# Attention times a token-mixing gate on one core: four closing adds moved to GpSimd, a clearing moved to VectorE, and another PSUM bank for the last span's sums

## The chip, the cores and the metric

The kernel runs on one core of a Trainium2 chip. The metric is the device time of one launch, in microseconds (us): the median of three timed runs was 1622.77 us before the change (1622.52 to 1623.23). The engines are TensorE (PE in the profile; its weight loads are PEld), VectorE (DVE), ScalarE (ACT), GpSimd (POOL) and the queue of SyncE (SP), from which nearly all transfers are started.

## What is computed

With S = 2048 tokens, D = 512 channels, 32 heads of 16 channels and a hidden size F = 1792 (all float32):

```python
xn = layernorm(x)
q, k, v = split(xn @ wqkv)                      # 32 heads of 16
s = concat_heads(softmax(q @ k.T * 16**-0.5) @ v) @ wo
h = layernorm(xn)
u = gelu(einsum("bsd,sf->bdf", h, w1) + b1)     # mixes tokens
y = einsum("bdf,fs->bds", u, w2) + b2
return x + s * silu(y.T)
```

## The kernel before the change

**Stages.** The first 200 us or so normalise x, make q, k and v, and begin the mixer. Then comes one long stretch in which attention and the mixer share TensorE. Attention runs over 16 pairs of heads; a pair has two spans of 1024 queries, and a span has 16 blocks of 128 keys. For each unit (a pair, a span and a key block) there are first row maxima (`max_of`, L524: a product on 48 rows, then a reduction on VectorE), and 22 units later the scores (`score`, L964): four products of 50 rows into a PSUM bank each, two for each head `a`, and ScalarE's exponential of each bank into a `prob` tile. Two units later `values` (L978) multiplies the unit's four `prob` tiles by the values (eight matmuls in the profile, 1 us in all) into one bank that sums over the 16 key blocks of a span; that bank's tile is `state["av"]`. `put_away` (L718) copies it to SBUF at the span's end. The two heads use the two halves of TensorE's rows, so their products run side by side.

**The fill.** Everything else that TensorE has to do is made by generators (`mixer`, L575, and `rest`, L995) that yield one product at a time, and a pair (work, give the bank back) at the end of each sum. `take(n, each)` (L1069) draws n of them for each step. Between yields the generators also start weight loads (`w_load`), split weights into two parts on GpSimd (`w_split`, L165 and L95) and load the mixer's results; so when a generator is advanced decides where these stand in their queues. Before the change `take` looked one item ahead after its last product, to see whether the end of a sum came next, and so advanced the generator then.

**The last 70 us.** When the last row maxima are done (`s == NU`, L1259, about 1550 us), the banks for scores (four) and for maxima (three) become one list of seven free banks, `Banks.free`. `Banks.tile` takes the first bank of the list and puts it at the end at once, so tiles rotate through what is on the list and a tile waits for the readers of the one that had the bank before; `Banks.hold` takes the first bank off the list until its second result, `back`, is called. The eighth bank is `ps_av`, in which the spans' sums stood. From there on each loop step has two half-steps (`a_half`, L1162): four scores, up to three products of the fill on each half of the rows, and then the values of an earlier unit. The fill's sums (tiles named `dn`) hold a bank each. The last products of the output projection (L1010 and on) finish the first eight of 16 blocks of rows in this stretch: `finish` (L953) multiplies a projection sum by the gate and adds the earlier part of the sum, y, on VectorE, and stores it. The pair's first span is turned with eight TensorE transposes (`own`, L831: L843 and L854, four each, into a `mx` bank).

**The close.** The last span's sums are copied by ScalarE (L725), turned (L1368), divided on VectorE into the cleared buffer `apart[0]` (`uo`, cleared by `clear_apart`, L869), turned back (`turn_back`, L1385), and split (`upper`, `lower`). Then come the last eight blocks, 8 to 15, in the order of `half`: 8, 9, 12, 13, 10, 11, 14, 15. For each, `product` (L1403) has three TensorE products, `gated` (L1409) multiplies by the gate, and `added` (L1411) adds y and stores. Block 15 goes in two halves (`in_parts`, L1419).

Blocks 8 and 9 (`SUMMED`) were different: their y was written straight to the output earlier (`store_y`, L911), and the gated sum was added to it there by a transfer started from GpSimd that accumulates (L1414). The y of the other blocks goes to `y_d` and comes back by `load_second` (L921, the transfer at L929) into `held`.

Of the kernel before, what the change touches and what calls it, by code (L numbers as in the profile page):

```python
# [9 lines left out]
F32 = mybir.dt.float32  # L10
F32R = mybir.dt.float32r
AF = mybir.ActivationFunctionType
OP = mybir.AluOpType
# [9 lines left out]
def tile_attention_token_mixer(ctx, tc, x, wqkv, wo, w1, b1, w2, b2, out):  # L23
    nc = tc.nc
    P = 128
# [4 lines left out]
    NP = H // 2  # L30
    NB = S // P
# [3 lines left out]
    QH = S // 1024  # L35
# [30 lines left out]
    ps_sc = Banks("ps_sc", 4)  # L66
    ps_mx = Banks("ps_mx", 3)
    ps_av = Banks("ps_av", 1)
# [649 lines left out]
    def put_away(p, span, av):  # L718

        ev = el.tile([P, 512], F32, name="ev")  # L720
        if p == NP - 1 and span < QH - 1:

            nc.vector.tensor_copy(ev, av)  # L723
        else:
            nc.scalar.copy(ev, av)  # L725
        if p == NP - 1:
            own(span, ev)
            return
        g, i = divmod(p, 4)
        if i == 0:  # L730
            dens[span] = sm.tile([P, 64], F32, name="d")
        rows = ev.rearrange("(j r) q -> r j q", r=32)
        for a in range(2):
            h = 2 * i + a
            nc.sync.dma_start(
                dens[span][DH * h : DH * (h + 1), :],
                rows[16 - 16 * a, 2 * a : 2 * a + 2, :].rearrange("c (j q) -> c j q", q=64),
            )
        nc.sync.dma_start(num_d[g][span][160 * i : 160 * i + P, :], ev)
        if i == 3 or p == NP - 2:  # L740
            invert(g, span)
# [125 lines left out]
    apart = []  # L867

    def clear_apart():  # L869

        apart.append(el.tile([P, 2, 512], F32, name="uo"))
        nc.gpsimd.memset(apart[0], 0.0)

    xts = {}
    gts = {}
# [1 line left out]
    gates = {}  # L877
    held = []
    PARTS = NB - 2
    LATE = NB - 4  # L880
    HALVES = 5
    SUMMED = range(NB // 2, NB // 2 + 2)

    def load_part(b):

# [7 lines left out]
    def part(b, ps):  # L893

        y = el.tile([P, D], F32, name="t", bufs=4)
        late = now[0] >= NU - 2
        if late:
            nc.vector.tensor_tensor(out=y, in0=ps, in1=gts[b], op=OP.mult)
        else:
            nc.scalar.copy(y, ps)  # L900

        def two():
            if not late:
                nc.gpsimd.tensor_tensor(out=y, in0=y, in1=gts[b], op=OP.mult)
            nc.gpsimd.tensor_tensor(out=y, in0=y, in1=xts[b], op=OP.add)
            load_part(b + 2)
            after(3, lambda: store_y(b, y))

        after(2, two)

    def store_y(b, y):  # L911
        if b in SUMMED:
            nc.sync.dma_start(out[b * P : (b + 1) * P, :], y)
            return
        nc.sync.dma_start(y_d[b], y)
        if b >= NB // 2:
            unkept.append(b)
# [3 lines left out]
    def load_second():  # L921

        b = next((b for b in unkept if b >= PARTS), min(unkept))
        unkept.remove(b)
        i = b - NB // 2
        while len(held) < NB // 8:
            held.append(big.tile([P, S], F32, name="big"))
        ys[b] = held[i // 4][:, i % 4 * 512 : i % 4 * 512 + 512]
        nc.sync.dma_start(ys[b], y_d[b] if b < PARTS else xv[:, b, :])  # L929
# [31 lines left out]
    state = {}  # L961
# [16 lines left out]
    def values(t):  # L978
        p, r = divmod(t, SPP)
        span, kb = divmod(r, NB)  # L980
        if kb == 0:
            state["av"] = ps_av.tile([P, 512], F32, name="av")
        av = state["av"]
        for a in range(2):
            for c in range(2):
                j = 2 * a + c
                nc.tensor.matmul(  # L987
                    av[32 * j : 32 * j + 32, :],
                    vps[p][:, kb, 16 * a : 16 * a + 32], prob.pop((t, a, c)),
                    start=kb == 0, stop=kb == NB - 1,  # L990
                )
        if kb == NB - 1:
            soon.append(lambda: put_away(p, span, av))
# [46 lines left out]
    def everything():  # L1040
        yield from mixer()
        yield from rest()

    class Fill:
# [10 lines left out]
        def next(self):  # L1055
            x = self.peek()
            self.ahead.clear()
            return x

    fill = Fill(everything())  # L1060
    open_ = True
# [7 lines left out]
    def take(n, each):  # L1069

        nonlocal open_, done
        got = 0
        while open_ and (got < n or fill.peek() and len(fill.peek()) == 2):
            x = fill.next()
            if x is False:
                open_ = False
            elif x is None:
                break
            elif len(x) == 2:
                def then(empty, back):  # L1080
                    empty()
                    back()

                each(None, lambda x=x: then(*x))
                if fill.peek() is None:
                    fill.next()
                    break
            else:
                each(x, None)
                got += 1  # L1090
        done += got

    def whole(x, then):
# [111 lines left out]
    def both_pairs(s, keep):  # L1205
# [5 lines left out]
        for i, kinds in enumerate((*zip(first, second), "")):  # L1211
# [14 lines left out]
            if then and not two:  # L1226
                then.pop()()

    take(FIRST, whole)
    after(5, lambda: load_v(0))  # L1230
    if NP > 1:
# [13 lines left out]
    def keep(s):  # L1245

        if done >= n_fill // 2 + 3 * NF:
            divisions()
        if s >= NU - SPP + LEAD and unkept:
            load_second()  # L1250

    for s in range(0, total + 1, 2):
# [16 lines left out]
        elif s < NU and t >= 0:  # L1269
# [6 lines left out]
            for i, kinds in enumerate((*zip(first, second), "")):  # L1276
                if i in places:

                    if i == places[0]:
                        piece()  # L1280
                    now[0] = s + places.index(i)
                    if now[0] >= LEAD + 2:
                        values(now[0] - LEAD - 2)
                    run_later()
                for of, kind in zip(made, kinds):
                    if of[kind]:
                        of[kind].pop(0)()
# [18 lines left out]
        else:  # L1306
# [13 lines left out]
            if s == NU + 16:  # L1320
                clear_apart()
# [9 lines left out]
        if 0 <= t < NT:  # L1331
            p, r = divmod(t, SPP)
# [23 lines left out]
    def some(n):  # L1356
        for f in beside[:n]:
            f()
        del beside[:n]
# [13 lines left out]
    for c in range(2):  # L1373
        for a in range(2):
            j = 2 * a + c
            nc.vector.tensor_tensor(
                out=spread[:, c, :, 96 + DH * a : 112 + DH * a], in0=turned[:, :, j, DH * a : DH * a + DH],
# [12 lines left out]
    def lower(h, c):  # L1390
        o = oc[ND - 1, 2 + c][96:, :, 256 * h : 256 * h + 256]
        sub(nc.vector, o[:, 1, :], back[h, c][96:, :256], o[:, 0, :])
# [3 lines left out]
    def product(n):  # L1396
        b = half[n]
        new = b not in sums
        if new:
            sums[b] = (ps_av if n == 0 else ps_sc).tile([P, 512], F32, name="av" if n == 0 else "sc")[:, :D]  # L1400
        o, at = oc[ND - 1, b // 4], cols[b % 4]
        for m, w in ((0, 0), (0, 1), (1, 0)):
            nc.tensor.matmul(sums[b], o[:, m, at], wide[w], start=new and m == 0 and w == 0, stop=m == 1)  # L1403

    def gated(n):
        b = half[n]
        g = gates[b]
        gates[b] = pp.tile([P, 512], F32, name="prob")[:, :D]
        nc.vector.tensor_tensor(out=gates[b], in0=sums[b], in1=g, op=OP.mult)  # L1409

    def added(n, eng):  # L1411
        b = half[n]
        if b in SUMMED:
            nc.gpsimd.dma_start(out[b * P : (b + 1) * P, :], gates[b], accum_op=OP.add)  # L1414
            return
        eng.tensor_tensor(out=gates[b], in0=ys[b], in1=gates[b], op=OP.add)
        nc.sync.dma_start(out[b * P : (b + 1) * P, :], gates[b])

    def in_parts(n):  # L1419
        b = half[n]  # L1420
        to = pp.tile([P, 512], F32, name="prob")[:, :D]
        for at in (slice(0, D // 2), slice(D // 2, D)):
            nc.vector.tensor_tensor(out=to[:, at], in0=sums[b][:, at], in1=gates[b][:, at], op=OP.mult)
            nc.vector.tensor_tensor(out=to[:, at], in0=ys[b][:, at], in1=to[:, at], op=OP.add)
            nc.sync.dma_start(out[b * P : (b + 1) * P, at], to[:, at])
# [11 lines left out]
        turn_back(1, c)  # L1437
        upper(1, c)
    lower(1, 0)
    adding = {0: [0], 1: [1], 3: [2], 4: [3], 5: [4], 6: [5, 6]}  # L1440
    for n in range(8):
        if n > 5:
            some(len(beside) if n == 7 else len(beside) - 9)
        product(n)
        if n == 7:
            in_parts(n)
            break
        gated(n)
        for i in adding.get(n, ()):
            added(i, nc.gpsimd if i in () else nc.vector)  # L1450
        if n == 1:
            lower(1, 1)

# [26 lines left out]
```

## Time and profile before

| what | us |
|---|---|
| median of three timed runs | 1622.77 |
| the profiled execution, its own time | 1621.93 |
| its span | 1620.0 |
| TensorE busy in the span | 1610.4 |
| VectorE busy | 1414.3 |
| ScalarE busy | 1192.3 |
| GpSimd busy | 552.4 |

The granted clock was 0.999 over the span. The profiled execution's own time is 1.93 us over its span and 0.84 us under the median of the runs. A row of the timeline has the start, the duration, the engine, the line, the operation and the tiles (out<-in), and in brackets the idle time before it with what ended that. Rows of matmuls have their shape as rows used by columns. Matmuls are pipelined: in a stream they start 0.23 us apart on each half of the rows, while each row says 0.39 us or more.

### The profile page before, as it was taken

Reading aid. Unit: us, or ns where it says so; the run is one execution under the profiler, and the core shown is the slowest. Engines: PE = TensorE matmul, PEld = TensorE weight load, DVE = VectorE, ACT = ScalarE, POOL = GpSimd, SP = SyncE. Lnnn points to the kernel's source line nnn. Section 1 sums busy time; section 2 is a strip of 40 time slices with the busy share of each in tenths; the row PEclk is TensorE's granted clock in tenths of the full one; section 3 lists DMA queues with packets and bytes.
Section 4 is the critical chain, followed back from the end, with each engine's and each line's share of the span. In section 5 each row is a group of like instructions: output and inputs, shape, how many; then the busy total and the mean of one; then the engine's idle time right before and its main releaser. Section 6 shows DMA issues by size and latency. Waiting matters only on the chain.

```text
span 1620.0 us, 31089 instructions
## 1 busy us (share of the span) xinstructions
PE 1610.4 (99%) x11899; PEld 876.2 (54%) x11899; DVE 1414.3 (87%) x2478; ACT 1192.3 (74%) x2306; POOL 552.4 (34%) x651
## 2 busy tenths in 40 slices
PE   9999999999999999999999999999999999999998
PEld 8888854554555554554454554544555545554544
DVE  7665999999999999999999999999999999999945
ACT  3333477777777777777877787777877777888885
POOL 1224844342244332332333332223232322563330
PEclk9999999999999999999999999999999999999999
DMA  7478441515133141826151522304150614444346
GB/s 231 178 249 200 120 93 41 96 39 78 41 68 75 27 79 40 241 71 109 41 83 37 85 59 42 69 31 76 38 86 31 113 32 80 112 99 131 111 136 222
DMA packets 151120, 153.34 MB, mean 95 GB/s; under 512 B 51372, under 2 KB 109996, under 8 KB 147900
## 3 DMA queue, kind: packets, MB, share of 16 engines
q1 hardware_dynamic: 146524, 150.25, 38.6%
q0 software_dynamic: 4448, 1.12, 0.5%
q8 instruction: 93, 1.52, 0.4%
q14 instruction: 55, 0.45, 0.1%
HBM read 99.63 MB, written 50.58 MB: 93 GB/s over the span
## 4 chain that ended last, share of the span: by engine, by line
PE 97%; DVE 1%; POOL 0%; issue 0%; ACT 0%; DMA 0%; SPq 0%; POOLq 0%; DVEq 0%
PE av L987 31%; PE dn L1132 23%; PE sc L971 17%; PE mx L533 14%; PE sc L436 3%; PE dn L672 2%; PE mx L436 2%; DVE mxp L537 1%; PE av L436 1%; PE dn L1178 0%; PE sc L104 0%; PE sc L102 0%; PE sc L103 0%; PE mx L340 0%; PE mx L102 0%; PE mx L104 0%
## 5 line engine op out<-in xcount | busy, mean ns | idle before, releaser
L537 DVE TENSOR_REDUCE mxp<-mx 128x1 f32<-128x512 f32 x2026 | 1250.3, 682 | 112.0 <-PE mx L533 85.7
L976 ACT ACTIVATE prob<-sc 128x512 f32<-128x512 f32 x2004 | 1039.7, 607 | 282.3 <-PE sc L971 116.5
L533 PE MATMUL mx<-big 48*128 48x512 f32 x2026 | 769.5, 419 | 0.1
L971 PE MATMUL sc<-big 50*128 50x512 f32 x2004 | 733.6, 412 | 0.5 <-ACT prob L976 0.5
L987 PE MATMUL av<-prob,vp 128*32 128x512 f32 x4096 | 545.5, 604 | 0.3 <-DVE ev L723 0.2
L1132 PE MATMUL dn<-hu,wh 64*128 64x512 f32 x1520 | 506.2, 404 | 0.0
L971 PEld LDWEIGHTS sc<-big 50*128 50x128 f32 x2004 | 353.9, 186 | 230.4 <-ACT prob L976 205.6
L533 PEld LDWEIGHTS mx<-big 48*128 48x128 f32 x2026 | 356.7, 185 | 196.0 <-DVE mxp L537 173.8
L1132 PEld LDWEIGHTS dn<-hu,wh 64*128 64x128 f32 x1520 | 272.1, 184 | 68.2 <-issue 45.3
L1132 PE MATMUL dn<-hu,wl 64*128 64x512 f32 x762 | 301.9, 396 | 0.0
L987 PEld LDWEIGHTS av<-prob,vp 128*32 128x32 f32 x4096 | 80.9, 108 | 176.3 <-issue 164.0
L95 POOL TENSOR_TENSOR wl<-raw,wh 128x512 fp32r<-128x512 f32 x124 | 150.7, 1218 | 64.0 <-ACT wh L167 22.6
L165 POOL CAST wh<-raw 128x512 fp32r<-128x512 f32 x104 | 60.4, 581 | 277.0 <-PE dn L1132 114.5
L1132 PEld LDWEIGHTS dn<-hu,wl 64*128 64x128 f32 x762 | 140.5, 184 | 11.6
L561 POOL CAST m<-f 16x128 fp32r<-16x128 f32 x31 | 8.7, 280 | 240.7 <-DVE f L549 240.7
L99 POOL DMA_DIRECT2D big<-m x124 | 65.6, 536 | 0.0
L622 POOL TENSOR_TENSOR sq<-u 128x512 f32<-128x512 f32 x11 | 11.5, 1041 | 133.7 <-ACT u L616 133.7
L1132 PE MATMUL dn<-wh,hu 64*128 64x512 f32 x144 | 51.0, 407 | 0.0
L709 POOL TENSOR_SCALAR t<-t 128x512 f32<-128x512 f32 x16 | 23.8, 1488 | 79.6 <-ACT t L706 79.5
L436 PE MATMUL sc<-xt,big 128*128 128x512 f32 x184 | 44.5, 390 | 0.0
L95 POOL TENSOR_TENSOR hu<-hx,hu 128x512 fp32r<-128x512 f32 x16 | 20.4, 1294 | 68.5 <-ACT hu L279 68.5
L672 PE MATMUL dn<-hu,wh 64*128 64x512 f32 x128 | 42.3, 392 | 0.0
(224 smaller groups left out, 1180.6 us busy)
## 6 DMA issues: line engine op xcount, KB each, us to landing
raw<-in_B_w_dram SPq DMA_DIRECT2D x104, 256.0 KB
big<-k_d SPq DMA_DIRECT2D x96, 128.0 KB
big<-q_d SPq DMA_DIRECT2D x96, 128.0 KB
q_d<-sg SPq DMA_DIRECT2D x16, 512.0 KB
k_d<-sg SPq DMA_DIRECT2D x16, 512.0 KB
num_d<-ev SPq DMA_DIRECT2D x30, 256.0 KB
u_d<-uo SPq DMA_DIRECT2D x14, 512.0 KB
hu<-u_d SPq DMA_DIRECT2D x14, 512.0 KB
```

Of the source, the lines that this page charges most:

```text
L95: eng.tensor_tensor(out=o, in0=a, in1=b.bitcast(F32), op=OP.subtract)
L99: queue.dma_start(dst.bitcast(F32), src.bitcast(F32))
L165: nc.gpsimd.tensor_copy(whs[n][:, :m, :], raws[n][:, :m, :])
L436: nc.tensor.matmul(ps, w[part][:, kd, m], xt[kd][:, z, :], start=w is wh and z == 0 and kd == 0, stop=w is wl and kd == ND - 1,)
L533: nc.tensor.matmul(ps, q[o : o + 48, r * P : (r + 1) * P], k[o : o + 48, c * 512 : (c + 1) * 512], start=True, stop=True,)
L537: nc.vector.tensor_reduce(mxp[u // 16][:, a, r % 8, c : c + 1], ps, axis=AX.X, op=OP.max)
L672: nc.tensor.matmul(ps, w(slice(0, 64)), m(slice(0, 64)), start=first, stop=last)
L709: nc.gpsimd.tensor_scalar(t, t, 1.0, None, op0=OP.add)
L971: nc.tensor.matmul(ps, ks[p][o : o + 50, kb * P : (kb + 1) * P], qs[p][o : o + 50, at : at + 512], start=True, stop=True,)
L976: nc.scalar.activation(e, ps, AF.Exp, scale=scale)
L987: nc.tensor.matmul(av[32 * j : 32 * j + 32, :], vps[p][:, kb, 16 * a : 16 * a + 32], prob.pop((t, a, c)), start=kb == 0, stop=kb == NB - 1,)
L1132: made.append(lambda r=r, start=first and a == lead, stop=last and a != lead: nc.tensor.matmul(ps, w(r), m(r), start=start, stop=stop,))
```

## The change

- `clear_apart`: VectorE clears the buffer in place of GpSimd.
- `SUMMED` is gone. The y of blocks 8 and 9 goes to `y_d` as that of the others does, and comes back by `load_second`; no transfer accumulates.
- `added` runs on GpSimd for the first four blocks of `half` (8, 9, 12, 13) and on VectorE for the next three (10, 11, 14). On VectorE, where there were five adds, there are three.
- The last span of the last pair takes the bank for its sums from the common list with `hold`, and never gives it back; the other spans keep `ps_av`. The first of the closing products still uses `ps_av`.
- `take` looks ahead only behind the product that ends a sum.
- `while not held or ...` does the same as before at these sizes.

```diff
     def clear_apart():
         apart.append(el.tile([P, 2, 512], F32, name="uo"))
-        nc.gpsimd.memset(apart[0], 0.0)
+        nc.vector.memset(apart[0], 0.0)
...
-    SUMMED = range(NB // 2, NB // 2 + 2)
...
     def store_y(b, y):
-        if b in SUMMED:
-            nc.sync.dma_start(out[b * P : (b + 1) * P, :], y)
-            return
         nc.sync.dma_start(y_d[b], y)
...
-        while len(held) < NB // 8:
+        while not held or len(held) < NB // 8:
...
         if kb == 0:
-            state["av"] = ps_av.tile([P, 512], F32, name="av")
+            last = p == NP - 1 and span == QH - 1
+            state["av"] = ps_sc.hold("dn")[0] if last else ps_av.tile([P, 512], F32, name="av")
...
         got = 0
-        while open_ and (got < n or fill.peek() and len(fill.peek()) == 2):
+        ended = False
+        while open_ and (got < n or ended and fill.peek() and len(fill.peek()) == 2):
...
                 each(x, None)
                 got += 1
+                ended = x[4]
...
     def added(n, eng):
         b = half[n]
-        if b in SUMMED:
-            nc.gpsimd.dma_start(out[b * P : (b + 1) * P, :], gates[b], accum_op=OP.add)
-            return
         eng.tensor_tensor(out=gates[b], in0=ys[b], in1=gates[b], op=OP.add)
         nc.sync.dma_start(out[b * P : (b + 1) * P, :], gates[b])
...
-    adding = {0: [0], 1: [1], 3: [2], 4: [3], 5: [4], 6: [5, 6]}
+    adding = {0: [0], 1: [1], 2: [2], 3: [3], 5: [4, 5], 6: [6]}
...
-            added(i, nc.gpsimd if i in () else nc.vector)
+            added(i, nc.gpsimd if i < 4 else nc.vector)
```

What stands where, engine by engine (lines in the rows of the changed kernel are its own, 1 to 4 less than before).

VectorE at the close before the change, from the third gated block on (`prob` tiles are the gated blocks 12, 13, 10, 11, 14 in this order, `big` holds y, `sc` and `dn` are the projection sums in PSUM, `hu` the gate):

```order
L1409 TENSOR_TENSOR prob_23314<-sc_23310,hu_20756 128x512
L1409 TENSOR_TENSOR prob_23320<-sc_23316,hu_20756 128x512
L1416 TENSOR_TENSOR prob_23314<-big_22187,prob_23314 128x512
L1409 TENSOR_TENSOR prob_23328<-sc_23324,hu_20546 128x512
L1416 TENSOR_TENSOR prob_23320<-big_22187,prob_23320 128x512
L1409 TENSOR_TENSOR prob_23336<-sc_23332,hu_20546 128x512
L1416 TENSOR_TENSOR prob_23328<-big_22186,prob_23328 128x512
L1409 TENSOR_TENSOR prob_23350<-dn_23252,hu_21173 128x512
L1416 TENSOR_TENSOR prob_23336<-big_22186,prob_23336 128x512
L1416 TENSOR_TENSOR prob_23350<-big_22187,prob_23350 128x512
```

and after it:

```order
L1408 TENSOR_TENSOR prob_23318<-sc_23314,hu_20756 128x512
L1408 TENSOR_TENSOR prob_23326<-sc_23322,hu_20756 128x512
L1408 TENSOR_TENSOR prob_23334<-sc_23330,hu_20546 128x512
L1408 TENSOR_TENSOR prob_23340<-sc_23336,hu_20546 128x512
L1412 TENSOR_TENSOR prob_23334<-big_22186,prob_23334 128x512
L1412 TENSOR_TENSOR prob_23340<-big_22186,prob_23340 128x512
L1408 TENSOR_TENSOR prob_23356<-dn_23254,hu_21173 128x512
L1412 TENSOR_TENSOR prob_23356<-big_22187,prob_23356 128x512
```

Two adds are gone from VectorE, and the products with the gate stand closer together. GpSimd at its end before the change (L905 adds x to y of the last blocks of the first part):

```order
L905 TENSOR_TENSOR t_22569<-t_22569,xt_22282 128x512
L905 TENSOR_TENSOR t_22892<-t_22892,xt_22451 128x512
L905 TENSOR_TENSOR t_22944<-t_22944,xt_22592 128x512
L872 MEMSET uo_23128 128x1024
L1414 DMA out_0_dram<-prob_23299 128x512
L1414 DMA out_0_dram<-prob_23306 128x512
```

and after it:

```order
L904 TENSOR_TENSOR t_22946<-t_22946,xt_22594 128x512
L1412 TENSOR_TENSOR prob_23301<-big_22186,prob_23301 128x512
L1412 TENSOR_TENSOR prob_23309<-big_22186,prob_23309 128x512
L1412 TENSOR_TENSOR prob_23318<-big_22187,prob_23318 128x512
L1412 TENSOR_TENSOR prob_23326<-big_22187,prob_23326 128x512
```

The clearing has left (on VectorE it stands between the fourth and the fifth `finish`), and four adds with both inputs in SBUF stand where two transfers were started.

TensorE at the last span's beginning before the change, with what each instruction waits for (scores `sc` and `mx`, then the values of the last span's first unit):

```order
L971 MATMUL sc_22796<-big_1481,big_1482 128x512 [waits Activation_49]
L971 MATMUL mx_22800<-big_1481,big_1482 128x512 [waits Activation_49]
L987 MATMUL av_22804<-prob_22760,vp_20943 32x512 [waits DVE_49]
L987 MATMUL av_22804<-prob_22765,vp_20943 32x512
L987 MATMUL av_22804<-prob_22773,vp_20943 32x512
```

and after it:

```order
L967 MATMUL sc_22798<-big_1481,big_1482 128x512 [waits Activation_49]
L967 MATMUL mx_22802<-big_1481,big_1482 128x512 [waits Activation_49]
L984 MATMUL dn_22806<-prob_22762,vp_20943 32x512 [waits Activation_49]
L984 MATMUL dn_22806<-prob_22767,vp_20943 32x512
L984 MATMUL dn_22806<-prob_22775,vp_20943 32x512
```

The wait for VectorE's copy of the first span's sums (L723) has become one for an exponential that last read the bank now taken. The order of TensorE's instructions is the same in both kernels, and so is ScalarE's. Earlier in the program some weight splits stand one step later on GpSimd, behind the small row-maximum operations (L561) or behind the two multiplications of L794, and the weight loads on SyncE's queue with them; two loads of y (blocks 8 and 9) are new on that queue, directly behind and between the stores of the same y.

## The prediction

> **What bounds the kernel now.** I read the page first, then TensorE's waits, then the last 70 us of the timeline, where all but one kind of edit acts.
>
> ```profile
> PE 1610.4 (99%) x11899; PEld 876.2 (54%) x11899; DVE 1414.3 (87%) x2478; ACT 1192.3 (74%) x2306; POOL 552.4 (34%) x651
> ```
>
> These are all the waits that TensorE's rows show in the whole span (engine, line, whom it waited for, us in total, times, longest):
>
> ```profile
> PE mx L340 <- POOL ident masks.py:199: 1.4, 1, 1.4
> PE sc L971 <- ACT prob L976: 0.5, 1, 0.5
> PE av L987 <- DVE ev L723: 0.2, 1, 0.2
> ```
>
> So TensorE sets the time from its start to its last product, and every transfer and every other engine is hidden under it there. What the change can win lies in the 0.2 us of the third row and behind TensorE's last product. What it can lose is any new wait of TensorE. The close looks like this: TensorE's last product, VectorE's chain, and the last store on SyncE's queue.
>
> ```profile
> 1612.22 0.39 PE L1403 MATMUL dn<-wh,hu 128*128 128x512 f32 x1
> ...
> 1610.34 0.68 DVE L1416 TENSOR_TENSOR prob<-big,prob 128x512 f32<-128x512 f32 x1
> 1610.94 0.69 DVE L1409 TENSOR_TENSOR prob<-sc,hu 128x512 f32<-128x512 f32 x1
> ...
> 1615.19 0.43 DVE L1424 TENSOR_TENSOR prob<-big,prob 128x256 f32<-128x256 f32 x1
> ...
> 1616.03 0.61 SPq L1425 DMA_DIRECT2D out_dram<-prob  x1
> ```
>
> TensorE is done at 1612.61 (1612.22 + 0.39), VectorE at 1615.62, the last transfer is issued at 1616.64, and the span ends at 1620.0. VectorE works without a gap, an operation each 0.60 us (1610.34 to 1610.94). At the end, then, VectorE is the bound, then the stores.
>
> **Part 1: the last span's bank.** The wait that goes:
>
> ```profile
> 1565.59 0.69 DVE L723 COPY ev<-av 128x512 f32<-128x512 f32 x1 [11.30 <-PE av L987]
> ...
> 1565.77 0.39 PE L971 MATMUL mx<-big 50*128 50x512 f32 x1
> 1566.33 1.06 PE L987 MATMUL av<-prob,vp 128*32 128x512 f32 x8 [0.17 <-DVE ev L723]
> ```
>
> The values start 0.05 us after VectorE's copy has ended (1566.28), and 0.56 us behind the last score; where nothing is waited for it is 0.33 us (1584.64 to 1584.97 below). So 0.23 us go.
>
> What comes: seven banks rotate, and from here on one of them is held to the end. I followed `Banks.free` by hand through both programs. While two projection sums are held (1566 to 1580), five banks are left to scores and turnings before, and four after. A half-step uses four banks, five with a turning, so a turning then takes the bank of the same half-step's first score. The two turnings and that score's exponentials:
>
> ```profile
> 1567.94 0.63 ACT L976 ACTIVATE prob<-sc 128x512 f32<-128x512 f32 x1
> ...
> 1568.68 0.66 PE L843 MATMUL mx<-ident,ev 128*128 128x128 f32 x4
> ...
> 1570.79 0.60 ACT L976 ACTIVATE prob<-sc 128x512 f32<-128x512 f32 x1 [0.75 <-PE mx L971]
> 1570.92 0.66 PE L854 MATMUL mx<-ident,t 128*128 128x128 f32 x4
> ```
>
> The first turning may not start before 1567.94 + 0.63 + 0.05 = 1568.62, so of the 0.23 us won only 0.06 are left. The second needs the exponential that ends at 1571.39; with 0.05 for the signal, and all of it 0.06 earlier, it starts at 1571.38 and not at 1570.92: 0.46 us lost, gain included. Two more fourth scores, near 1577.6 and 1579.2, need an exponential of the half-step before that ends about as they start: 0 to 0.4 us together; I take 0.2.
>
> Then the eight `finish` half-steps. Three sums are held when the first two scores are drawn (the third is given back before the third score). Before, four banks are on the list then, and the fourth score gets the bank of the previous half-step's fourth. After, three are on the list, and in six half-steps running (of the first six `finish` sums) **the fourth score gets the bank of the same half-step's first**. One such half-step as it is now:
>
> ```profile
> 1583.61 0.50 PE L971 MATMUL sc<-big 50*128 50x512 f32 x1
> 1583.94 0.39 PE L971 MATMUL sc<-big 50*128 50x512 f32 x1
> ...
> 1584.14 0.60 ACT L976 ACTIVATE prob<-sc 128x512 f32<-128x512 f32 x1 [0.29 <-PE dn L1178]
> ...
> 1584.41 0.39 PE L971 MATMUL mx<-big 50*128 50x512 f32 x1
> 1584.64 0.39 PE L971 MATMUL mx<-big 50*128 50x512 f32 x1
> 1584.97 1.07 PE L987 MATMUL av<-prob,vp 128*32 128x512 f32 x8
> ```
>
> The first score's exponential ends at 1584.74. The fourth score could start at 1584.79 and stands at 1584.64 now: 0.15 us. Its weight load is then no longer hidden: behind a restart the next product comes after 0.33 us (1583.61 to 1583.94), in the stream after 0.23 (1584.41 to 1584.64), so up to 0.25. The values stand behind it on TensorE. I take 0.20: 6 x 0.20 = 1.2 us (0.9 to 1.5). ScalarE does not hide it, it is what is waited for.
>
> Part 1: 0.46 + 0.2 + 1.2 = **+1.9 us** (1.4 to 2.4).
>
> **Part 2: who adds.** Two operations of 0.60 us leave VectorE's chain. Its product with the gate for block 14 must then wait for TensorE (about 1611.75 against 1611.54), which leaves some 1.0 us; the fifth projection product, whose bank is now the one that the last `lower` reads, takes 0.15 of that: -0.85 us, if VectorE runs freely. But it runs beside GpSimd, and these rows say what that can mean:
>
> ```profile
> 1551.38 1.28 POOL L95 TENSOR_TENSOR hu<-sq,hu 96x512 fp32r<-96x512 f32 x1
> 1552.63 1.26 POOL L905 TENSOR_TENSOR t<-t,xt 128x512 f32<-128x512 f32 x1
> ...
> 1551.87 2.11 DVE L561 CAST m<-f 16x128 fp32r<-16x128 f32 x1
> ```
>
> ```profile
> L95 DVE TENSOR_TENSOR m<-f,m 16x128 fp32r<-16x128 f32 x1 | 0.3, 280 | 0.0
> 15.62 0.81 DVE L95 TENSOR_TENSOR big<-wl,big 128x512 fp32r<-128x512 f32 x1
> 16.34 0.68 DVE L95 TENSOR_TENSOR big<-raw,big 128x512 fp32r<-128x512 f32 x1
> 14.58 1.29 POOL L95 TENSOR_TENSOR big<-wh,big 128x512 fp32r<-128x512 f32 x1
> 1548.13 1.28 POOL L905 TENSOR_TENSOR t<-t,xt 128x512 f32<-128x512 f32 x1
> 1548.75 0.68 DVE L898 TENSOR_TENSOR t<-dn,gt 128x512 f32<-128x512 f32 x1
> ```
>
> A conversion of 16x128, a shape that takes 0.28 us next to it, lasted 2.11 us and ended 0.09 us behind the second of two GpSimd operations in a row. A VectorE operation with both inputs in SBUF took 0.81 where the next took 0.68; it ended 0.56 us behind the GpSimd operation that was running. With one input in PSUM (L898) nothing happened. In the close the products with the gate read PSUM, but the adds have both inputs in SBUF. GpSimd's four adds start when the first gated block is there:
>
> ```profile
> 1606.07 0.69 DVE L1409 TENSOR_TENSOR prob<-av,hu 128x512 f32<-128x512 f32 x1
> ```
>
> From 1606.80 on, a new one each 1.25 us (1551.38 to 1552.63), the last ends at 1606.80 + 3 x 1.25 + 1.28 = 1611.83. If VectorE's first add, ready at 1610.34, is kept out till then, it ends 0.56 us later, at 1612.4; two adds, a product and the halves follow, and the chain ends near 1615.8, **+0.2 us** against now. If each of two adds is only stretched by the 0.13 of the row at 15.62, it is -0.6. I take +0.2, because GpSimd's operations stand in a row as at 1551.38; -0.85 stays the lower end.
>
> The Trainium skill, on the page "SBUF — State Buffer", section "Who interferes with whom", says that a VectorE instruction with two SBUF inputs contends with a GpSimd instruction that reads SBUF, and that the holder keeps the shared ports for its whole instruction. By that rule the sum takes the +0.2, without it the -0.85; the rows at 1551.87 and 15.62 agree with it.
>
> **Part 3: stores.** Two transfers started by GpSimd go, two plain stores come, early in the close. The last two stores now are slow to issue: 0.61 us against the 0.33 of an undisturbed one, and the last starts 0.41 us after its data are there (1615.62).
>
> ```profile
> 1611.05 0.33 SPq L1417 DMA_DIRECT2D out_dram<-prob  x1
> 1617.00:1618.00 1.00, 0.00 (x0) 0.00 (x0) 0.00 (x0) 0.00 (x0) 0.00 (x0) 0.78 1.04 388
> ```
>
> The transfer engines are full then (the last columns are their share and GB/s). With earlier stores these two delays go, 0.41 + 0.28 = 0.7 us: **-0.7** (-1.2 if the queue empties faster too, -0.2 if the full engines stay the limit). GpSimd's stores stand ahead of VectorE's on the queue; the fourth is ready at 1611.9 and costs 0.33 each, so block 10's waits for it, under VectorE's chain.
>
> **Part 4: nothing.** The clearing on VectorE stands in a gap of 0.89 us behind the fourth `finish`; no row shows it there. Half of its size copied takes 0.43 us and an operation on it 0.69, so 0.9 to 1.4 us. The next `finish` slips by up to 0.4 us and catches up in the next gap; without the gap it would cost TensorE 0.4 through the bank. The page "VectorE: DVE Perf Modes" of the Trainium skill, section "Zero memsets can be issued as uint32 (trn2)", gives one cycle per element, an estimate of 1.07 us at its 0.96 GHz; by that it is the same. The new loads of y can hold SyncE's queue for a landing (up to 2.5 us, below), at a place where it is idle from 1537.4 to 1549.4. The later weight splits come behind waits of up to 18.5 us; TensorE waits for no weights now, and they are split several chunks ahead.
>
> ```profile
> SPq L929 <- DMA y_d<-t: 4.8, 3, 2.5
> 1536.96 0.45 SPq L913 DMA_DIRECT2D out_dram<-t  x1
> 1549.44 0.34 SPq L889 DMA_DIRECT2D xt<-in_A_x_dram  x1
> POOL m L561 <- DVE f L549: 240.7, 28, 18.5
> ```
>
> **Sum.** 1.9 + 0.2 - 0.7 = +1.4 us on the profiled execution's 1621.93. The median of the runs is 0.84 higher; the difference carries over, so 1622.8 + 1.4 = **1624.2 us**. About 0.2% (3.2 us) is what a measurement of this kernel can tell from no change; so the forecast is no change, on the slow side. Bounds: 1.4 - 0.85 - 1.2 = -0.65 to 2.4 + 0.3 - 0.2 = +2.5.
>
> **Rivals.**
>
> A. *The banks are free in time.* If the exponentials' end releases a bank earlier than I read it, or the fourth score slips into ScalarE's 0.29 us of idle time at no cost, part 1 is -0.2, the adds give -0.85 and the stores -0.7 to -1.2: -1.8 to -2.3, 1620.5 to 1621.0 us. For it: TensorE shows one wait on ScalarE in 1620 us. Against: that was with one bank more. Without the contention of part 2 alone the sum is 1623.1.
>
> B. *Slower: the bank waits feed on themselves.* Where ScalarE runs without a gap an exponential starts 0.60 us behind its score or later, not 0.53, and a TensorE that is late bunches the scores. If each of nine waits (the turning, two fourth scores, six in the `finish` half-steps) costs the 0.5 us of the one wait on record, part 1 is +4.5, and with +0.2 and -0.7 it is +4.0: 1626.8 us. It decides from 0.4 us a wait on, where the sum passes 3.2. For it:
>
> ```profile
> 1554.00:1566.00 12.00, 12.00 (x92) 4.55 (x90) 0.69 (x2) 11.99 (x24) 0.00 (x0) 1.00 0.70 228
> 1582.00:1596.00 14.00, 14.00 (x109) 5.95 (x108) 8.30 (x12) 12.23 (x25) 0.00 (x0) 1.00 0.85 290
> ```
>
> ScalarE (fourth busy column) is busy for 11.99 of 12 us there. Against it: 12.23 of 14 where the six waits are.
>
> C. *Weights come late.* A split behind an 18.5 us wait reaches TensorE's chunk too late: some us, 1625 to 1630. Against: no such wait now.
>
> **How the numbers follow.** The forecast has 0.56, A 0.26, B 0.12, C 0.06. A could reach 0.2% with a luckier close (0.04 of its share); B is slower by over 0.2%, C in a third of its cases. Faster 0.04, same 0.82, slower 0.14. The range goes from 1620.8 (most of A) to 1626.3 (the forecast's end, some of C, short of B).
>
> **What would show it.** Right: waits of the fourth score (L967 there) on ScalarE, some 0.2 us in each `finish` half-step, 0.4 to 0.5 us at the second turning, a period of 2.55 us instead of 2.36; VectorE's first add of the close well over 0.69 us, ending about 0.6 behind GpSimd's last; no wait on L723. Wrong: TensorE's close starting within 0.3 us of before, or any wait of TensorE ahead of 1560.

## The result and the profile after

The changed kernel is slower: 1627.81 us (median of seven runs, 1626.73 to 1628.84) against 1622.77, a ratio of 1.0033 with a 95% interval of 1.0024 to 1.0042. The forecast was 1624.2 us in a range of 1620.8 to 1626.3, so it missed by 3.6 us and by 1.5 us outside the range. The profiled execution took 1627.49 us with a span of 1625.7, 5.7 us over the span before.

The page of the changed kernel says how much each engine worked, and that is the same as before within 2.3 us for every engine. TensorE's waits follow it:

```profile
PE 1611.9 (99%) x11899; PEld 878.1 (54%) x11899; DVE 1415.5 (87%) x2477; ACT 1192.6 (73%) x2306; POOL 554.6 (34%) x652
```

```profile
PE mx L340 <- POOL ident masks.py:199: 1.4, 1, 1.4
PE sc L356 <- ACT xt L318: 0.6, 1, 0.6
PE mx L854 <- ACT prob L972: 0.5, 1, 0.5
PE sc L356 <- POOL wvh L211: 0.2, 1, 0.2
```

The wait for VectorE's copy is gone, and the second turning (L854) waits 0.5 us for an exponential, as forecast. (The two waits at L356 are in the first 12 us, where both kernels have the same instructions. By the letter they are a sign of being wrong that the prediction names, a wait ahead of 1560 us; but they differ from profile to profile, from none in kernels 5, 7 and 11 below to 0.9 us in kernel 4, and are not put down to the change.) The six waits of the fourth scores don't show there, because a product whose weights are late is put down to its weight load. They are in the waits of the weight loads, in a row that the kernel before doesn't have:

```profile
PEld mx L967 <- ACT prob L972: 1.4, 6, 0.3
```

Six waits, 1.4 us. Two of these half-steps, the first one with the exponential that is waited for (the first of a group of two, over at 1585.40); the fourth score starts 0.44 us behind the third, where it was 0.23:

```profile
1584.80 1.09 ACT L972 ACTIVATE prob<-sc 128x512 f32<-128x512 f32 x2 [0.59 <-PE dn L1177]
1585.01 0.40 PE L967 MATMUL mx<-big 50*128 50x512 f32 x1
1585.45 0.49 PE L967 MATMUL mx<-big 50*128 50x512 f32 x1
1585.87 1.06 PE L984 MATMUL dn<-prob,vp 128*32 128x512 f32 x8
...
1587.67 0.40 PE L967 MATMUL mx<-big 50*128 50x512 f32 x1
1588.05 0.50 PE L967 MATMUL mx<-big 50*128 50x512 f32 x1
1588.48 1.06 PE L984 MATMUL dn<-prob,vp 128*32 128x512 f32 x8
```

The values stand 2.61 us apart here, and 2.66 or 2.67 us in the half-steps beside them. Before they were 2.36 apart (1584.97, in the prediction, to this row of the kernel before):

```profile
1587.33 1.06 PE L987 MATMUL av<-prob,vp 128*32 128x512 f32 x7
```

That is the forecast loss, somewhat larger than forecast, and it is not what the forecast lacked most. The close of the changed kernel, GpSimd's and VectorE's adds and the last stores:

```profile
1608.89 1.29 POOL L1412 TENSOR_TENSOR prob<-big,prob 128x512 f32<-128x512 f32 x1 [28.94 <-DVE prob L1408]
...
1611.40 1.30 POOL L1412 TENSOR_TENSOR prob<-big,prob 128x512 f32<-128x512 f32 x1
1612.35 0.89 DVE L1412 TENSOR_TENSOR prob<-big,prob 128x512 f32<-128x512 f32 x1
1612.65 1.74 POOL L1412 TENSOR_TENSOR prob<-big,prob 128x512 f32<-128x512 f32 x1
1613.17 1.77 DVE L1412 TENSOR_TENSOR prob<-big,prob 128x512 f32<-128x512 f32 x1
...
1617.43 0.43 DVE L1420 TENSOR_TENSOR prob<-big,prob 128x256 f32<-128x256 f32 x1
1617.88 0.33 SPq L1421 DMA_DIRECT2D out_dram<-prob  x1
```

The last two of these rows are the last of any engine in the timeline: VectorE ends at 1617.85 and the last store is issued at 1618.21, 7.5 us ahead of the span's end. Before, the last issue ended 3.4 us ahead of it. What happens in between is seen in the windows (busy time of TensorE, its weight loads, VectorE, ScalarE and GpSimd; the last two columns are the transfer engines' share and GB/s):

```profile
1616.00:1618.00 2.00, 0.00 (x0) 0.00 (x0) 1.79 (x5) 0.00 (x0) 0.00 (x0) 1.00 1.02 379
1618.00:1620.00 2.00, 0.00 (x0) 0.00 (x0) 0.00 (x0) 0.00 (x0) 0.00 (x0) 0.87 0.41 140
1620.00:1622.00 2.00, 0.00 (x0) 0.00 (x0) 0.00 (x0) 0.00 (x0) 0.00 (x0) 0.50 0.00 0
1622.00:1624.00 2.00, 0.00 (x0) 0.00 (x0) 0.00 (x0) 0.00 (x0) 0.00 (x0) 0.50 0.00 0
1624.00:1625.70 1.70, 0.00 (x0) 0.00 (x0) 0.00 (x0) 0.00 (x0) 0.00 (x0) 0.50 0.00 0
```

From 1620 on nothing works and nothing is transferred, for 5.7 us. Somebody waits, and the waits of SyncE's queue have it, at the line that ends the program. First the row of the kernel before, then that of the changed one:

```profile
SPq L1476 <- PEq L1476: 0.7, 2, 0.5
```

```profile
SPq L1472 <- PEq L1472: 5.4, 2, 4.9
```

SyncE waits 4.9 us at the barrier of the engines. The releaser in these rows ("PEq") is an inference. The trace's own records of the closing DRAIN instructions, which no view counts as busy, name another: each engine ends with such an instruction, SyncE's is done at 1620.21, and GpSimd's lasts until 1624.94, **10.55 us behind the end of GpSimd's last add**. In the kernel before GpSimd's drain was over at 1617.35, 5.48 us behind the end of the instruction that started its second accumulating transfer (1611.87), and 1.85 us ahead of SyncE.

| in the profiled runs, us | forecast | measured |
|---|---|---|
| TensorE's last product ends | +1.9, and 0.15 counted in part 2 | 1612.61 to 1614.88: +2.27 |
| VectorE's chain ends | +2.1 in all | 1615.62 to 1617.85: +2.23 |
| from there until SyncE is done | -0.7 | 3.58 to 2.36: -1.22 |
| SyncE is done | +1.4 in all | 1619.20 to 1620.21: +1.01 |
| from there until GpSimd's drain ends | not in the sum | 0 to 4.73: +4.73 |
| span | +1.4 | +5.7 |

Up to the last landing, the sum holds to 0.4 us, in part by luck: TensorE lost 0.4 us more behind 1560 us than the sum has, and the stores won 0.5 us more. The loss that it does not contain lies behind the last landing.

### The profile page after: what moved, and what is told of

Its sections match the earlier page's. It is cut to its first block, busy times and chain, and to the rows that moved or that the text cites. A ratio compares the mean times of both kernels' runs of the same rounds, so it can differ in the third digit from the quotient of the medians.

```text
span 1625.7 us, 31087 instructions
## 1 busy us (share of the span) xinstructions
PE 1611.9 (99%) x11899; PEld 878.1 (54%) x11899; DVE 1415.5 (87%) x2477; ACT 1192.6 (73%) x2306; POOL 554.6 (34%) x652
## 4 chain that ended last, share of the span: by engine, by line
PE 96%; DVE 1%; ACT 1%; DMA 1%; POOL 0%; issue 0%; SPq 0%; POOLq 0%; DVEq 0%; ACTq 0%
PE av L984 30%; PE dn L1131 24%; PE sc L967 16%; PE mx L533 13%; PE sc L436 3%; PE dn L672 2%; PE mx L436 2%; PE dn L984 1%; DVE mxp L537 1%; PE av L436 1%; ACT prob L972 0%; PE dn L1177 0%; PE mx L967 0%; PE sc L102 0%; PE sc L104 0%; PE sc L103 0%
## 5 line engine op out<-in xcount | busy, mean ns | idle before, releaser
L984 PE MATMUL av<-prob,vp 128*32 128x512 f32 x3968 | 528.2, 605 | 0.2
L561 POOL CAST m<-f 16x128 fp32r<-16x128 f32 x31 | 8.7, 282 | 245.2 <-DVE f L549 245.2
```

The costliest lines, as they stand in the source:

```text
L984: nc.tensor.matmul(av[32 * j : 32 * j + 32, :], vps[p][:, kb, 16 * a : 16 * a + 32], prob.pop((t, a, c)), start=kb == 0, stop=kb == NB - 1,)
```

## The experiments

Theory D: GpSimd's closing drain, a fixed time behind its last add, ends the program; the bank waits delay all that stands ahead of it by some 2.2 us. The rivals are that the bank waits carry nearly all of the loss (rival B of the prediction), and that the empty stretch belongs to the stores or to the program's end itself.

The table has, from each profiled run, what GpSimd's last instruction was and when it ended, when GpSimd's drain ended, when SyncE was done, the span, and the median of the runs. For a transfer start, "behind it" counts from the end of the instruction that starts the transfer. Runs 1 to 4 shared one chip (kernel before there 1622.75), 5 to 8 another (1622.48), 9 to 11 a third (1622.43); each ratio is to the kernel before on the same chip, and medians of different chips are compared only roughly.

| kernel | GpSimd's last | drain ends | behind it | SyncE done | span | median |
|---|---|---|---|---|---|---|
| before | transfer start, 1611.87 | 1617.35 | 5.48 | 1619.20 | 1620.0 | 1622.77 |
| changed | add, 1614.39 | 1624.94 | 10.55 | 1620.21 | 1625.7 | 1627.81 |
| 1 first span's bank | add, 1613.26 | 1623.81 | 10.55 | 1619.09 | 1624.6 | 1625.94 |
| 2 all adds on VectorE | add (L904), 1580.34 | 1590.89 | 10.55 | 1621.41 | 1622.2 | 1624.21 |
| 3 two adds | add, 1611.79 | 1622.33 | 10.54 | 1620.29 | 1623.1 | 1625.32 |
| 4 eight banks | add, 1612.71 | 1623.26 | 10.55 | 1618.54 | 1624.0 | 1625.44 |
| 5 one column | copy, 1617.28 | 1627.83 | 10.55 | 1620.71 | 1628.6 | 1630.93 |
| 6 two adds, start last | transfer start, 1615.46 | 1617.88 | 2.42 | 1620.75 | 1621.5 | 1623.91 |
| 7 eight banks, one add | add, 1609.30 | 1619.84 | 10.54 | 1619.51 | 1620.6 | 1621.47 |
| 8 small edits alone | transfer start, 1611.75 | 1617.27 | 5.52 | 1619.12 | 1619.9 | 1622.02 |
| 9 eight banks, two adds, start last | transfer start, 1612.80 | 1615.24 | 2.44 | 1618.08 | 1618.9 | 1621.27 |
| 10 eight banks, three adds, start last | transfer start, 1614.42 | 1617.35 | 2.93 | 1618.53 | 1619.3 | 1621.03 |
| 11 changed, start last | transfer start, 1618.24 | 1620.67 | 2.43 | 1620.59 | 1621.5 | 1623.32 |

In each row the span ends 0.8 us behind the later of GpSimd's drain and SyncE.

**1, the first span's bank.** The bank change alone is undone.

```diff
-            state["av"] = ps_sc.hold("dn")[0] if last else ps_av.tile([P, 512], F32, name="av")
+            state["av"] = ps_av.tile([P, 512], F32, name="av")
```

> The changed kernel with one part undone: the last span's sums are back in the bank of the first span's. Theory D (GpSimd's closing drain, which ends 10.5 us behind its last add, ends the program; the bank waits delay everything ahead of it by 2.2 us): TensorE's close starts 2.2 us earlier, GpSimd's last add too, and the gap between that add and the end of the span stays 11.3 us; time 1627.8 - 2.2 = 1625.6 us. Rival B (the bank waits carry nearly all of the loss, through the close): 1622.8 us or a little less.

1625.94 us, ratio to before 1.0021 (1.0012 to 1.0030). The change's bank costs 1.9 us by the medians, about what its waits say (this kernel has none of the six nor the one at the second turning, and waits 0.2 us for the copy again), and 3.2 us are left that it has nothing to do with. Rival B falls: the bank waits are not nearly all of the loss.

**2, all adds on VectorE.**

```diff
-    adding = {0: [0], 1: [1], 2: [2], 3: [3], 5: [4, 5], 6: [6]}
+    adding = {1: [0], 2: [1], 3: [2], 4: [3], 5: [4], 6: [5, 6]}
...
-            added(i, nc.gpsimd if i < 4 else nc.vector)
+            added(i, nc.vector)
```

> The changed kernel with all seven whole adds on VectorE, GpSimd has nothing to do in the last 40 us. Theory D: the empty stretch of some 5 us at the end, behind the last landing, goes, and the span ends about 1 us behind the last landing as in the kernel before; VectorE's chain has 2 operations of 0.60 us more than before and starts 2.0 us later, so the last landing is near 1621.5 and the time near 1624.4 us (1623.8 to 1625.2). Rival (the empty stretch has to do with the stores or with the program's end itself): it stays about 5 us, 1628 to 1629 us.

1624.21 us, ratio 1.0009 (1.0000 to 1.0018). VectorE's chain has four operations more than in the changed kernel and ends 1.39 us later (1619.24), and the kernel is 3.6 us faster. The wait at the end is what it was before:

```profile
SPq L1472 <- PEq L1472: 0.7, 2, 0.5
```

The stores are the same, in the same order, as in the changed kernel, so the empty stretch does not belong to them.

**3, two adds.** Blocks 8 and 9 on GpSimd, 12 and 13 back on VectorE.

```diff
-    adding = {0: [0], 1: [1], 2: [2], 3: [3], 5: [4, 5], 6: [6]}
+    adding = {0: [0], 1: [1], 3: [2], 4: [3], 5: [4], 6: [5, 6]}
...
-            added(i, nc.gpsimd if i < 4 else nc.vector)
+            added(i, nc.gpsimd if i < 2 else nc.vector)
```

> The changed kernel with two adds on GpSimd (blocks 8 and 9) and five on VectorE. Theory D: GpSimd's last add ends near 1611.4, 3.0 us earlier than in the changed kernel, and the span ends 3.0 us earlier, still by GpSimd: 1624.8 us. Rival 1 (the drain has a price per GpSimd operation): half of the delay goes too, 1622.5 to 1623.5. Rival 2 (any GpSimd work in the close ends the span at the same place): 1627.8.

1625.32 us (0.5 us over the forecast), ratio 1.0018 (1.0009 to 1.0026). The last add ends 2.60 us earlier and so does the drain: a price by the place of the last add, not by their number.

**4, eight banks.** The first span's bank joins the list when the last span takes one from it, and the first closing product draws from the list too.

```diff
             state["av"] = ps_sc.hold("dn")[0] if last else ps_av.tile([P, 512], F32, name="av")
+            if last:
+                ps_sc.free.append(ps_av.free[0])
...
-            sums[b] = (ps_av if n == 0 else ps_sc).tile([P, 512], F32, name="av" if n == 0 else "sc")[:, :D]
+            sums[b] = ps_sc.tile([P, 512], F32, name="sc")[:, :D]
```

> The changed kernel with one bank more in the list: when the last span takes its bank from the list, the first span's bank joins it, so that as many banks rotate as in the kernel before. If the waits of the fourth scores and of the second turning come from the count of banks, TensorE has none of them and its close starts 2.2 to 2.4 us earlier; GpSimd's drain still ends the span 11.3 us behind its last add: 1625.4 to 1625.6 us. If they come from something else (the new bank's place in the order, the adds), TensorE stays as late: 1627.8.

1625.44 us, ratio 1.0017 (1.0008 to 1.0026). TensorE's waits on ScalarE at the second turning and the fourth scores are gone, and so is the one for the copy. These are all that its rows show:

```profile
PE mx L340 <- POOL ident masks.py:199: 1.4, 1, 1.4
PE sc L356 <- ACT xt L318: 0.7, 1, 0.7
PE sc L356 <- POOL wvh L211: 0.2, 1, 0.2
PE mx L313 <- DVE xn L255: 0.2, 1, 0.2
```

The last span still takes its bank from the list here, so the waits came from the count of banks that rotate and not from taking one there. The drain still ends the span.

**5, one column.** Kernel 2 with an operation that no result needs: GpSimd copies a column of the last whole block.

```diff
+            nc.gpsimd.tensor_copy(apart[0][:, 0, :1], gates[half[6]][:, :1])
```

> The kernel with all adds on VectorE, and one more GpSimd operation that no result needs: a copy of a 128x1 column, behind VectorE's last whole add (near 1618). If any arithmetic on GpSimd, however small, holds its closing drain for 10.5 us: the drain ends near 1628.7 and the time is 1631 to 1632 us, 7 us over the kernel without the copy (1624.2). Rival (the 10.5 us belong to the 128x512 adds, their size or their data): within 1 us of 1624.2.

1630.93 us, ratio to before 1.0050 (1.0037 to 1.0064), and 6.7 us over kernel 2 (6.4 us by the spans of the profiles). An operation of 0.19 us that nobody waits for does this. Its row, and SyncE's wait at the end:

```profile
1617.10 0.19 POOL L1448 COPY uo<-prob 128x1 f32<-128x1 f32 x1 [37.43 <-DVE prob L1412]
```

```profile
SPq L1474 <- PEq L1474: 7.8, 2, 7.3
```

The drain ends 10.55 us behind it, as behind a 128x512 add.

**6, a transfer started last.** Kernel 3, with the store of GpSimd's second block started from GpSimd.

```diff
-        nc.sync.dma_start(out[b * P : (b + 1) * P, :], gates[b])
+        (nc.gpsimd if n == 1 else nc.sync).dma_start(out[b * P : (b + 1) * P, :], gates[b])
```

> The kernel with two adds on GpSimd, the store of the second started from GpSimd and not from SyncE, so that GpSimd's last instruction is the start of a transfer, as in the kernel before (where its drain ended 5.5 us behind that). Theory 1 (the 10.5 us run from the last arithmetic, whatever follows): the drain ends as it did with both stores on SyncE, 1625.3 us. Theory 2 (only the last instruction counts): it ends near 1618.5, the stores end the span, 1623.0 to 1623.6 us.

1623.91 us (kernel 3: 1625.32); ratio to before 1.0008 (0.9999 to 1.0017). The drain is over 6.30 us behind the add's end (1611.58) and not 10.55, though a transfer was started in between. Theory 1 of the expectation falls, and theory 2 is nearer, though the time is 0.3 us over its range: what stands last counts.

**7, eight banks and one add.** Kernel 4 with block 8's add on GpSimd and six on VectorE.

```diff
-    adding = {0: [0], 1: [1], 2: [2], 3: [3], 5: [4, 5], 6: [6]}
+    adding = {0: [0], 2: [1], 3: [2], 4: [3], 5: [4], 6: [5, 6]}
...
-            added(i, nc.gpsimd if i < 4 else nc.vector)
+            added(i, nc.gpsimd if i < 1 else nc.vector)
```

> Eight banks in the rotation, block 8's add on GpSimd, the other six on VectorE, no accumulating transfer. GpSimd's add ends near 1608.1 and its drain near 1618.7, no later than the last landing; VectorE has one operation of 0.60 us more than the kernel before, TensorE is 0.2 us earlier, the last stores issue 0.7 us sooner: 1622.1 us (1621.7 to 1622.6) against 1622.75. If the price of a GpSimd operation in the close does not hang on its place, it stays near 1624 to 1625.

1621.47 us (0.2 us under the range), ratio 0.9994 (0.9985 to 1.0003): not told apart from before. One add costs 0.3 us where four cost 4.7 us, since the drain is over hardly later than SyncE (1619.84 against 1619.51).

**8, the small edits alone.** The kernel before, with VectorE clearing the buffer and the shorter look ahead of `take`.

```diff
-        nc.gpsimd.memset(apart[0], 0.0)
+        nc.vector.memset(apart[0], 0.0)
...
-        while open_ and (got < n or fill.peek() and len(fill.peek()) == 2):
+        ended = False
+        while open_ and (got < n or ended and fill.peek() and len(fill.peek()) == 2):
...
                 got += 1
+                ended = x[4]
```

> The kernel before with the two small edits alone: VectorE clears the buffer, and the fill looks ahead only behind the end of a sum. Forecast of the prediction's part 4: no change, 1622.8 us (1622.3 to 1623.3), no wait of TensorE for weights. Rival C (weights late): 1624 or more.

1622.02 us (0.3 us under the range), ratio 0.9999 (0.9990 to 1.0008): no change that the runs can tell, and behind the first 12 us no wait of TensorE for weights.

**9 and 10, versions that avoid both costs.** Eight banks, two and three adds on GpSimd, and the last one's store started from GpSimd. The diff is that of kernel 4 with, for three adds (kernel 9 has the table of kernel 3, `i < 2` and `n == 1`):

```diff
-        nc.sync.dma_start(out[b * P : (b + 1) * P, :], gates[b])
+        (nc.gpsimd if n == 2 else nc.sync).dma_start(out[b * P : (b + 1) * P, :], gates[b])
...
-    adding = {0: [0], 1: [1], 2: [2], 3: [3], 5: [4, 5], 6: [6]}
+    adding = {0: [0], 1: [1], 2: [2], 4: [3], 5: [4], 6: [5, 6]}
...
-            added(i, nc.gpsimd if i < 4 else nc.vector)
+            added(i, nc.gpsimd if i < 3 else nc.vector)
```

> Eight banks in the rotation, two adds on GpSimd (blocks 8 and 9), the second's store started from GpSimd, five adds on VectorE. If a transfer started behind the last add ends the drain 6.3 us behind that add (as in the run with two adds and GpSimd's store), the drain is over near 1615.8 and the stores end the span: VectorE's chain as in the kernel before less 0.2, 1621.4 us (1620.9 to 1622.0). If the drain lasts 10.5 us from the add: 1620 plus what lies around, 1622.8.

> As the run with eight banks and two adds, with block 12's add on GpSimd too and its store started from GpSimd; four adds on VectorE. One operation of 0.60 us less on VectorE, drain over near 1617: 1620.9 us (1620.3 to 1621.8). If VectorE's first add is held out by GpSimd's third, the 0.60 us are lost again: 1621.5.

1621.27 us, ratio 0.9994 (0.9985 to 1.0003), and 1621.03 us, ratio **0.9990 (0.9981 to 0.9999)**. The interval of the second lies just below 1; as one of eleven such comparisons that is weak evidence that it is faster than the kernel before. It is faster than the changed kernel by 6.8 us (6.4 us by the spans). VectorE's first add in it shows the contention again:

```profile
1609.60 1.49 DVE L1414 TENSOR_TENSOR prob<-big,prob 128x512 f32<-128x512 f32 x1
1611.01 0.68 DVE L1410 TENSOR_TENSOR prob<-sc,hu 128x512 f32<-128x512 f32 x1
```

**11, the changed kernel with one store moved.** Only the store of GpSimd's fourth block is started from GpSimd and not from SyncE.

```diff
-        nc.sync.dma_start(out[b * P : (b + 1) * P, :], gates[b])
+        (nc.gpsimd if n == 3 else nc.sync).dma_start(out[b * P : (b + 1) * P, :], gates[b])
```

> The changed kernel with one edit: the store of GpSimd's fourth block is started from GpSimd. Nothing else moves, GpSimd's last add ends near 1614.4 as there. If the end of the changed kernel hangs on how long GpSimd's drain lasts behind its last instruction (10.5 us behind arithmetic, some 6.3 us behind an add that a started transfer follows), the drain ends near 1620.7 and the time is 1623.6 us (1623.0 to 1624.3). If it hangs on the work that GpSimd does there, it stays at 1627.8 or above.

1623.32 us, ratio to before 1.0006 (0.9997 to 1.0014). That is 4.5 us below the changed kernel's median, and 4.2 us below by what each loses against the kernel before on its own chip (0.9 and 5.0 us). TensorE, VectorE and the adds end where they did (1614.85, 1617.82, 1614.36). The row of the store, and SyncE's wait at the end:

```profile
1617.59 0.65 POOL L1413 DMA_DIRECT2D out_dram<-prob  x1 [3.23 <-issue]
```

```profile
SPq L1472 <- PEq L1472: 0.7, 2, 0.5
```

The added work on GpSimd is all there, and 4.2 to 4.5 us of the 5.0 lost are gone; the drain ends 4.27 us earlier. That is the plainest evidence for theory D, with one thing added to it: the loss hangs on what GpSimd's last instruction is, and when it ends.

## Why the prediction was wrong

**What bounds the close: the step that failed.** "At the end, then, VectorE is the bound, then the stores." That held for the kernel before. But the program ends when every engine's closing drain is over, and GpSimd's was a third candidate with only 1.85 us of slack. The change replaced two transfer starts at GpSimd's end by adds. The prediction followed GpSimd's adds to 1611.83 and asked what they do to VectorE, and never asked when GpSimd itself is done. None of its rivals has this term, and it measured 4.73 us. The 10.55 us could not be read at the close of the trace of before, since there the drain stood behind transfer starts; but the record of that drain was in it, from 1610.47 to 1617.35, and it was reason enough to bound the term.

**Part 1, the bank: right in mechanism, and 2.2 us instead of 1.9.** The wait on the copy is gone and won 0.24 us (forecast 0.23). The second turning starts 0.48 us later than it would have, gain included (0.46):

```profile
1570.59 0.60 ACT L972 ACTIVATE prob<-sc 128x512 f32<-128x512 f32 x1 [0.69 <-PE mx L967]
...
1571.24 0.66 PE L854 MATMUL mx<-ident,t 128*128 128x128 f32 x4 [0.45 <-ACT prob L972]
```

The two fourth scores behind it set TensorE's values back by 0.05 us (0.2), and the six in the `finish` half-steps by 1.70 (1.2, in bounds of 0.9 to 1.5). These numbers compare the start of the same product in both kernels. In the six, the fourth scores themselves start 0.15 to 0.21 us later, as forecast, but the values stand 0.42 us behind a fourth score that waited (1585.45 to 1585.87), where the prediction let them follow at 0.33: that 0.1 us each time is what it mis-sized. Kernels 1 and 4 show the cause from two sides. Rival A, banks free in time, falls; of rival B the six waits exist, at 0.28 us each and not 0.5.

**Part 2, the adds: right in size, and in the main in mechanism.** VectorE's two adds that met GpSimd's ended at 1613.24 and 1614.94, 0.54 and 0.55 us behind GpSimd's third and fourth (1612.70 and 1614.39); the prediction had read 0.56. But it had the first add kept out until GpSimd's last was over, and a sign of being right was that add at well over 0.69 us; it came in behind the third and took 0.89 us, and it was the second that took 1.77. The chain moved by 0.1 us more than forecast, with TensorE. The rule of the Trainium skill ("SBUF — State Buffer", "Who interferes with whom") agrees with these pairs and with the one of kernel 10 (1611.09 against 1610.54). What it costs GpSimd was not in the sum: its fourth add took 1.74 us instead of 1.29, and the drain starts from its end.

**Part 3, the stores: right in sign, at the end of its bounds.** -1.22 us, where -0.7 was taken and -1.2 was the bound. The last store is issued at once and in 0.33 us, which gives the 0.7; the other 0.56 are that SyncE is done 2.00 us behind the end of that issue, where it was 2.56. In kernel 8, which keeps the accumulating transfers, SyncE is done 3.6 us behind VectorE's end as before; in kernels 1 to 4 it takes 2.2 to 2.4.

**Part 4: right as far as the runs can tell.** Kernel 8 has no change. But one of the waits of TensorE that the prediction shows, the 0.5 us on ScalarE at L971 (1550.39), stands in the profile of before and in none of the twelve others. In kernel 8 TensorE's rows gain 0.49 us there against before, in the changed kernel 0.47, so the shorter look ahead of `take` was not nothing for TensorE. The likely reason, not shown, is that advancing a generator also draws the next sum's bank from the list, and so changes which bank the waiting score gets. In the changed kernel's profile this gain hides a delay of 0.3 us from its first 100 us, which differs from profile to profile.

In the changed kernel the clearing took 0.91 us in its gap, less than the prediction's estimate of 1.07, and the `finish` behind it was not late:

```profile
1592.12 0.91 DVE L872 MEMSET uo<- 128x1024 f32 x1 [0.16 <-issue]
1593.14 0.69 DVE L951 TENSOR_TENSOR t<-dn,hu 128x512 f32<-128x512 f32 x1
...
1595.82 0.69 DVE L951 TENSOR_TENSOR gt<-dn,gt 128x512 f32<-128x512 f32 x1 [1.26 <-PE dn L1177]
```

The loads of y held SyncE's queue for up to 6.3 us at once, more than the 2.5 taken, and TensorE waited for nothing there:

```profile
SPq L925 <- DMA y_d<-t: 11.9, 4, 6.3
```

## What to carry to other kernels

Before work is moved to an engine near the end of a program, look up when each engine is done, its closing drain in the raw records included, and give that end a term of its own: an idle engine is not free there. Here GpSimd's last arithmetic had to end 10.5 us ahead of the moment at which SyncE was done, so one add cost 0.3 us, four cost 4.7 us, and a transfer started behind the fourth won 4.2 to 4.5 back. A bank that is held to the end costs what the rotation loses, and a bank that falls idle at the same moment can be put in its place.

## What the runs showed of the hardware

- GpSimd's closing drain ended 10.54 or 10.55 us behind the end of its last arithmetic in all seven kernels where arithmetic stood last, behind adds of 128x512 and a copy of 128x1 alike. In kernel 2 it ran its 10.55 us in the middle of the program, and cost nothing.
- With a transfer start last, the drain ended 2.4 to 2.9 us behind the end of that instruction when an add stood directly ahead of it (kernels 6, 9, 10 and 11), and 5.5 us behind that of the second accumulating transfer in the kernel before and kernel 8. The start itself began 3.23 us behind the add whose data it stores, in all four kernels, where SyncE's stores in the changed kernel were issued 0.03 us behind theirs. From the add's end to the drain's end it is 6.3 to 6.8 us.
- Why the drain lasts this long, and why a transfer start shortens it, was not settled: the runs show when it ends, not what it does.
